# Retention attention with routed experts: routing intermediates in PSUM, the order of early weights, and the last two accumulating scatters

## The chip, the cores and the metric

One core of one Trainium2 chip runs the kernel, in one launch. The metric is device time in microseconds (us), lower is better. Engines carry the names of the profile: PE is TensorE, DVE is VectorE, ACT is ScalarE, POOL is GpSimd, SP is SyncE, which here only issues DMAs.

## The reference

```python
def _attn_ref(q, k, v):                      # (8, 8, 576, 64) each
    B, H, S, D_ = q.shape
    scores = 1.0 / np.sqrt(D_) * np.matmul(q, k.transpose(0, 1, 3, 2))
    gamma = 1.0 - 2.0 ** (-5.0 - np.arange(H, dtype=np.float32))
    rel = np.arange(S)[:, None] - np.arange(S)[None, :]
    Dmat = np.where(rel >= 0, gamma[:, None, None] ** rel[None, :, :], 0.0)
    return np.matmul(scores * Dmat[None], v)

def _moe_ref(x, w_gate, w_noise, noise, w1, w2):   # x (4608, 512), 8 experts, F = 1024
    noisy = x @ w_gate + np.log1p(np.exp(x @ w_noise)) * noise
    top2 = np.argpartition(-noisy, 2, axis=1)[:, :2]
    top2_w = softmax(noisy[top2])                  # over the two
    for e in range(8):
        for k in range(2):
            mask = top2[:, k] == e
            out[mask] += top2_w[mask, k, None] * (np.maximum(x[mask] @ w1[e], 0) @ w2[e])
```

The attention output, token by token, is `x` of the second part.

## The kernel before, in words

Nothing is scheduled by hand line by line. The class `Plan` holds a list of operations; each names its engine (or a choice of engines) with a cost in microseconds, what it reads and writes, and a priority. `Plan.run` simulates the engines with those costs and picks again and again the operation that can start first; among those that could start at the same time the lower `prio` goes first. Buffers are taken from pools in that simulation too. The outcome is one fixed order of instructions on each engine. On the chip every engine follows its order strictly: an instruction whose input is late holds everything behind it on that engine.

**Attention.** Sixteen units `u`, four for each pair of batches `bp`. `load` and `load_tail` fetch float32 q, k, v by DMAs that SP issues, `cast` scales and casts them to bf16 (k on ACT or DVE, line 501 or 503; q and v on DVE or POOL, lines 510 and 517), `tr` transposes on PE, `scores` and `states` multiply, `out_` finishes. `tail` handles the last 64 tokens of each batch.

**Routing.** After the four units of a pair, `route(bp)` computes the gates of its 1152 tokens on columns of 9, finds the two best experts, ranks tokens within each expert, and builds the table `xi` of token rows by expert: two one-hot tensors `olo` (18 x 128) and `oh` (18 x 80), made by comparing an iota with `lof` and `hif` (line 846), `oh` scaled by `vals` (849), and 18 matmuls (854). All its small tensors lie in SBUF, and some of its operations may go to POOL (the lists `DP` and `DC`). It also writes x with its gate values (`pay`) to `xd` in DRAM (line 886, issued by SP).

**Experts.** A piece is 128 rows of one expert (the tenth is 64). `tiles` closes 15 of the 80 pieces early, out of the tokens of the first three pairs (`CLOSE`), so that they can run while attention goes on; they are the tiles with `up` (line 1070) and the matmuls of line 1158. The other tiles, four pieces at most, follow in the main stage (`wide`, lines 1096 and 1158, the second matmul of one tile between the first ones of the next). `fetch` gathers rows of `xd` (POOL, line 993) two tiles ahead and transposes them on PE (line 1015), or by DMA transposes that SP issues (line 1005) from expert 5 on. `finish` scales the sum by its gate value (ACT at line 1192 or DVE at 1194) and scatters rows to the output (POOL, line 1198): a plain write for the lower-numbered of a token's two experts, an accumulating one for the other. Every token gets exactly these two. All of expert 7's rows are of the second sort, and its pieces 9 (64 rows) and 8 (128 rows), in this order, are the last tile.

**Weights.** Those of experts 0, 1 and 2 are cast by POOL's own DMAs (`weights` with `cast_dma`, lines 926 and 930), into space in which attention's raw inputs lay; `WAIT` names the unit whose loads must have landed first, and the priorities are 40, 41 and 42. Those of the other experts come as float32 through SP's DMAs (lines 940 and 943) and are cast by ACT or DVE (lines 282 and 284).

Two details of the end: before the last tile's finish there is a `drain` of POOL (line 1307), and behind everything a loop over tokens without room (`overflow`), which here runs zero times.

Of the kernel before, what the change touches and what calls it, by code (L numbers as in the profile page):

```python
# [17 lines left out]
P = 128  # L18
# [32 lines left out]
class Op:  # L51
    __slots__ = ("i", "eng", "fn", "prio", "dma", "port", "preds", "succ", "need", "allocs", "bufs", "fin", "on", "pace", "slack", "hold")


class Plan:
# [22 lines left out]
    def op(self, eng, cost, fn, r=(), w=(), prio=0.0, dma=0, after=(), port=False, pace=0.0, slack=0.0, hold=0.0):  # L78
        o = Op()
        o.i, o.fn, o.prio, o.dma, o.port, o.pace, o.slack, o.hold = len(self.ops), fn, prio, dma, port, pace, slack, hold  # L80
        o.eng = eng if isinstance(eng, dict) else {eng: cost}
# [30 lines left out]
    def run(self):  # L112
# [35 lines left out]
        while ready:  # L148
            pick = None
            for o in ready:  # L150
# [92 lines left out]
class Kernel:  # L243
# [47 lines left out]
    def setup(self):  # L291
# [87 lines left out]
        vals = f("vals", [P, 2 * C9, 2], F16)  # L379
        o("POOL", 0.2, vals, lambda: G.iota(vals.t.rearrange("p (j c) x -> p j c x", j=2), pattern=[[0, 2], [P, C9], [0, 2]],  # L380
# [10 lines left out]
        early = f("early", [P, 3, E])  # L391
# [3 lines left out]
        for e in range(E):  # L395
# [4 lines left out]
            for k in range(3):  # L400
                z(early, (k, e), early.t[:, k, e:e + 1], float(CLOSE[k][e] - FIRST[e]))
# [83 lines left out]
    def cast(self, u):  # L485
# [18 lines left out]
        for c in range(2):  # L504
            pl.op({"ACT": 0.63, "DVE": 0.43}, 0, lambda e, c=c: k(e, c), r=[(rk[c], x4)], w=[(kn, c)], prio=u, port=True)
# [217 lines left out]
    def route(self, bp, prio):  # L723
# [7 lines left out]
        def o(e, cost, fn, r, w, prio=prio):  # L731
            two = not {"tensor_reduce", "reciprocal", "tensor_single_scalar"} & set(fn.__code__.co_names)
# [8 lines left out]
        gv = lambda: pg.t[:, :C * 2 * E].rearrange("p (c e) -> p c e", c=C)  # L741

# [8 lines left out]
        nl = f("nl", [P, C, E])  # L751
        o("ACT", 0.23, lambda e: nc.scalar.activation(nl.t, gv()[:, :, E:], Act.Exp), [pg], [nl])
        o("ACT", 0.3, lambda e: nc.scalar.activation(nl.t, nl.t, Act.Ln, bias=1.0), [nl], [nl])
        o(DC, 0, lambda e: self.eng(e).tensor_tensor(nl.t, nl.t, nz.t[:, bp], Alu.mult), [nl, nz], [nl])
        o("DVE", DV, lambda e: V.tensor_add(nl.t, nl.t, gv()[:, :, :E]), [nl, pg], [nl])
# [6 lines left out]
        w = lambda j: keep_w.t[:, j, c0:c0 + C]  # L762

        def first_max(src, name):
            m, s, x = f(name + "m", [P, C]), f("scr", [P, C, E]), f(name + "w", [P, C])
            o("DVE", DV, lambda e: V.tensor_reduce(m.t, src.t, AX, Alu.max), [src], [m])
            o("DVE", DV, lambda e: V.tensor_tensor(s.t, src.t, bc(m.t), Alu.is_ge), [src, m], [s])
            o(DC, 0, lambda e: self.eng(e).tensor_tensor(s.t, s.t, dsc(), Alu.mult), [s, desc], [s])
            o("DVE", DV, lambda e: V.tensor_reduce(x.t, s.t, AX, Alu.max), [s], [x])
            return m, x  # L770

        m1, w1 = first_max(nl, "a")
        M1, nl2 = f("M1", [P, C, E]), f("nl2", [P, C, E])
        o("DVE", DV, lambda e: V.tensor_tensor(M1.t, dsc(), bc(w1.t), Alu.is_equal), [w1, desc], [M1])
        o("DVE", DV, lambda e: V.scalar_tensor_tensor(nl2.t, M1.t, -1.0e30, nl.t, Alu.mult, Alu.add), [M1, nl], [nl2])
        m2, w2 = first_max(nl2, "b")
# [4 lines left out]
        kw = [(keep_w, (bp, 0)), (keep_w, (bp, 1))]  # L781
        o("DVE", 0.3, lambda e: V.tensor_tensor(
            MM.t, desc.t.unsqueeze(1).unsqueeze(1).to_broadcast(sh),
            keep_w.t[:, :, c0:c0 + C].unsqueeze(3).to_broadcast(sh), Alu.is_equal), kw + [desc], [MM])

        d, r, x, df = f("d", [P, C]), f("r", [P, C]), f("low1", [P, C]), f("df", [P, C])
        pay = f(f"pay{bp % 2}", [P, C, PLW])
        tok = self.fixed["tok"]
        sub = lambda e, o_, a, b, op: self.eng(e).tensor_tensor(o_, a, b, op)
        o(DP, 0, lambda e: sub(e, d.t, m2.t, m1.t, Alu.subtract), [m1, m2], [d])  # L790
        o("ACT", 0.22, lambda e: nc.scalar.activation(d.t, d.t, Act.Exp), [d], [d])
        o(DP, 0, lambda e: self.eng(e).tensor_scalar_add(r.t, d.t, 1.0), [d], [r])
        o("DVE", DV, lambda e: V.reciprocal(r.t, r.t), [r], [r])
        o(DP, 0, lambda e: sub(e, d.t, d.t, r.t, Alu.mult), [d, r], [d])
        o("DVE", DV, lambda e: sub(e, x.t, w1.t, w2.t, Alu.is_gt), [w1, w2], [x])
        o(DP, 0, lambda e: sub(e, df.t, r.t, d.t, Alu.subtract), [r, d], [df])
        o(DP, 0, lambda e: sub(e, df.t, df.t, x.t, Alu.mult), [df, x], [df])
        o(DP, 0, lambda e: sub(e, pay.t[:, :, 0], d.t, df.t, Alu.add), [d, df], [(pay, 0)])
        o(DP, 0, lambda e: sub(e, pay.t[:, :, 1], r.t, df.t, Alu.subtract), [r, df], [(pay, 1)])
        o(DP, 0, lambda e: self.eng(e).tensor_copy(pay.t[:, :, 2].bitcast(I32), tok.t[:, bp]), [tok], [(pay, 2)])  # L800
# [4 lines left out]
        def ranks(e):  # L805
# [5 lines left out]
        o("PE", 0.9, ranks, [MM, ltri, ones], [pr])  # L811
        base, bnd, early = self.fixed["base"], self.fixed["bnd"], self.fixed["early"]
        ub, bt = f("ub", [P, 2, C, E]), f("bt", [P, 2, C])
        o(DP, 0, lambda e: self.eng(e).tensor_tensor(ub.t, MM.t, bnd.t.unsqueeze(2).to_broadcast(sh), Alu.mult), [MM, bnd], [ub])
        o("DVE", 0.3, lambda e: V.tensor_reduce(bt.t, ub.t, AX, Alu.add), [ub], [bt])
        u = f("u", [P, 2, C, E])
        o("DVE", 0.3, lambda e: V.tensor_tensor(u.t, rv()[:, :, :C, :], base.t.unsqueeze(2).to_broadcast(sh), Alu.add),
          [pr, base], [u])
        o("DVE", DV, lambda e: V.tensor_tensor(base.t, base.t, rv()[:, :, C, :], Alu.add), [pr, base], [base])
        if bp < 3:  # L820
            o("DVE", DV, lambda e: V.tensor_tensor(base.t[:, 0], base.t[:, 0], early.t[:, bp], Alu.max), [base, early], [base])
        o("DVE", 0.3, lambda e: V.tensor_tensor(u.t, u.t, MM.t, Alu.mult), [u, MM], [u])
        t = lambda: keep_t.t[:, :, c0:c0 + C]
        kt = (keep_t, bp)
        o("DVE", 0.3, lambda e: V.tensor_reduce(t(), u.t, AX, Alu.add), [u], [kt])
# [603 lines left out]
```

## Time and profile before

| | us |
|---|---|
| median of 3 runs (lowest to highest) | 442.14 (441.96 to 443.67) |
| the profiled execution: its time, its span | 438.85, 437.2 |
| PE busy in the span | 378.9 |
| POOL, ACT, DVE busy | 298.1, 263.3, 161.9 |
| mean granted clock of TensorE | 0.955 |

The span runs from the first to the last instruction. Spans and busy times are from one profiled execution, which was 3.29 us below the median of the runs. Rows of the profile give the line of the kernel, the engine, the operation, what it writes and reads, its duration, and in brackets how long the engine had been idle before it and which instruction's end it had been waiting for.

### The profile page before, as it was taken

The page shows a single profiled execution, that of the slowest core. Times are in us where ns is not written, and L with a number is a line of the kernel's source. Part 1 is how long each engine was busy: PE and PEld are TensorE (multiplying, and loading weights), DVE is VectorE, ACT ScalarE, POOL GpSimd, SP SyncE. Part 2 cuts the span into 40 slices and gives each one's busy share as a digit, 9 for nine tenths or more (in the row PEclk, how much of TensorE's full clock was granted, in tenths as well). Part 3 has the DMA queues.
Part 4 walks back from the last instruction along what each step waited for, and adds up shares of the span by engine and source line. Part 5 has one row for each costly group of instructions (what it writes and reads, how often), then busy time and mean ns, then how long its engine had stood idle before and what let it go on. Part 6 is the DMA issues. An engine that isn't in the chain of part 4 may idle for free. (4 is left out here: it accounts for less than half of the span.)

```text
span 437.2 us, 11020 instructions
## 1 busy us (share of the span) xinstructions
PE 378.9 (87%) x4312; PEld 240.4 (55%) x4312; DVE 161.9 (37%) x425; ACT 263.3 (60%) x450; POOL 298.1 (68%) x344
## 2 busy tenths in 40 slices
PE   2787686585989699999899898999999899999991
PEld 1675575574767567675465444554554454454460
DVE  4755489877477968002063403121102100000000
ACT  4688597744978454666657464465755464555451
POOL 8773787593489857575566667686786776783653
PEclk9999698876999699999999999999999999999997
DMA  8997999999993999973689859459999999697586
GB/s 236 300 259 172 312 266 259 309 263 251 286 266 59 235 230 205 343 273 114 251 288 311 264 154 273 145 106 251 176 290 197 291 187 166 125 135 114 74 108 81
DMA packets 99960, 94.26 MB, mean 216 GB/s; under 512 B 36799, under 2 KB 77248, under 8 KB 99906
## 3 DMA queue, kind: packets, MB, share of 16 engines
q1 hardware_dynamic: 82114, 58.08, 48.3%
q0 software_dynamic: 17792, 35.46, 40.4%
q8 instruction: 34, 0.56, 0.5%
q14 instruction: 20, 0.16, 0.1%
HBM read 72.32 MB, written 26.36 MB: 226 GB/s over the span
## 5 line engine op out<-in xcount | busy, mean ns | idle before, releaser
L1158 PE MATMUL ps<-W,half 128*128 128x512 bf16 x576 | 186.2, 379 | 2.9 <-ACT half L1079 2.6
L1096 PE MATMUL ps<-big,W 128*128 128x512 bf16 (+4 forms) x640 | 182.5, 329 | 0.0
L1079 ACT ACTIVATE half<-ps 128x512 bf16<-128x512 f32 (+5 forms) x188 | 93.5, 504 | 95.3 <-PE ps L1096 79.9
L1198 POOL DMA_INDIRECT out_dram<-half,xg x74 | 97.7, 1320 | 43.1 <-ACT half L1192 14.3
L993 POOL DMA_INDIRECT xg<-xd,xi x80 | 84.3, 1054 | 59.6 <-issue 15.6
L1158 PEld LDWEIGHTS <-half 128*128 128x128 bf16 x576 | 55.8, 98 | 63.0 <-ACT half L1079 3.3
L1096 PEld LDWEIGHTS <-W 128*128 128x128 bf16 x640 | 62.5, 98 | 46.4 <-issue 1.0
L1192 ACT ACTIVATE half<-ps,xg 128x512 f32<-128x512 f32 (+1 forms) x58 | 39.3, 678 | 12.9 <-PE ps L1158 11.6
L1194 DVE TENSOR_SCALAR half<-ps,xg 64x256 f32<-64x256 f32 (+1 forms) x24 | 14.0, 591 | 89.1 <-ACT half L1079 40.5
L572 DVE TENSOR_TENSOR half<-ps,mask 128x512 bf16<-128x512 f32 x64 | 40.1, 681 | 15.3 <-PE ps L564 11.4
L282 ACT ACTIVATE half<-ps 128x1024 bf16<-128x1024 bf16 (+1 forms) x35 | 34.8, 1011 | 12.3 <-PE ps L533 4.9
L284 DVE CAST W<-big 128x1024 bf16<-128x1024 f32 x25 | 17.2, 735 | 64.6 <-PE ps L1168 28.9
L1070 PE MATMUL ps<-half,W 128*128 128x256 bf16 (+1 forms) x288 | 29.9, 260 | 4.5 <-DVE half L284 4.4
L1070 PEld LDWEIGHTS <-W 128*128 128x128 bf16 x288 | 24.6, 99 | 8.5 <-issue 4.7
L282 ACT ACTIVATE tb<-ps 64x512 bf16<-64x512 f32 x32 | 18.9, 591 | 15.1 <-PE ps L597 14.9
L282 ACT ACTIVATE xT<-ps 128x512 bf16<-128x512 f32 (+1 forms) x37 | 18.6, 553 | 9.8 <-PE ps L642 6.7
L1015 PE MATMUL ps<-ident__61,xg 128*128 128x128 bf16 (+1 forms) x200 | 17.6, 219 | 4.8 <-DMA xg<-xd,xi 4.8
L597 PE MATMUL ps<-half,half 64*64 64x64 bf16 (+2 forms) x512 | 19.6, 228 | 2.3 <-POOL half L517 2.3
L533 PE MATMUL ps<-ident__61,half 128*128 128x128 bf16 x128 | 12.5, 255 | 10.2 <-POOL half L510 7.2
L564 PE MATMUL ps<-half,half 64*64 64x128 bf16 x512 | 12.9, 244 | 9.1 <-ACT half L282 8.8
L1015 PEld LDWEIGHTS <-xg 128*128 128x128 bf16 (+1 forms) x200 | 13.0, 98 | 12.5 <-DMA xg<-xd,xi 5.3
L597 PEld LDWEIGHTS <-half 64*64 64x64 bf16 (+1 forms) x512 | 16.6, 123 | 5.7 <-issue 3.6
(171 smaller groups left out, 444.9 us busy)
## 6 DMA issues: line engine op xcount, KB each, us to landing
big<-in_moe_w_dram SPq DMA_DIRECT2D x40, 512.0 KB, 7.3
W<-in_moe_w_dram POOLq DMA_DIRECT2D x12, 512.0 KB
xd<-xg SPq DMA_DIRECT2D x16, 264.0 KB, 6.3
W<-in_q_dram SPq DMA_DIRECT2D x16, 256.0 KB, 5.0
big<-in_k_dram SPq DMA_DIRECT2D x8, 512.0 KB, 5.8
big<-in_v_dram SPq DMA_DIRECT2D x8, 512.0 KB, 8.1
big<-in_q_dram SPq DMA_DIRECT2D x16, 256.0 KB, 7.1
W<-in_k_dram SPq DMA_DIRECT2D x6, 512.0 KB, 6.3
```

Of the source, the lines that this page charges most:

```text
L282: self.nc.scalar.activation(out, in_, Act.Copy)
L284: self.eng(e).tensor_copy(out, in_)
L572: nc.vector.tensor_tensor(S.t.bitcast(BF16).rearrange("p (h c x) -> p h c x", h=2, c=2)[:, h], p[h].t.rearrange("p (c x) -> p c x", c=2), ...
L597: nc.tensor.matmul(o[h * HD:(h + 1) * HD, hp, n, :], lhsT=kk[:k, r, c, y], rhs=vv[:k, r, c, y].unsqueeze(1).to_broadcast([k, n.stop - n.st ...
L993: ins = nc.gpsimd.indirect_dma_start(out=x.t[:n, :], out_offset=None, in_=self.xd[:rows, :], in_offset=IOff(ap=xi.t[:n, h:h + 1], axis=0), ...
L1015: nc.tensor.transpose(pv()[:, di, a:a + n], xb[:, di * P:(di + 1) * P], ident.t[:n, :n])
L1070: nc.tensor.matmul(pv()[:, f2, :], lhsT=w.t[:, o:o + P], rhs=xv()[:, di, :n], start=(di == 0), stop=(di == KD - 1))
L1079: self.nc.scalar.activation(o, i, Act.Relu)
L1096: self.mm = nc.tensor.matmul(p.t[:, :n], lhsT=w.t[:, o:o + P], rhs=xv()[:, di, :n], start=(di == 0), stop=(di == KD - 1))
L1158: self.mm = self.nc.tensor.matmul(po.t, lhsT=hv[:, c:c + P], rhs=self.W[e].t[:, o:o + DM], start=(f == 0), stop=(f == KF - 1))
L1192: nc.scalar.activation(y.t[:n, c], x, Act.Copy, scale=g()[:n])
L1198: ins = nc.gpsimd.indirect_dma_start(out=self.out[:, :], out_offset=IOff(ap=ix()[:n], axis=0), in_=y.t[:n, :], in_offset=None, bounds_chec ...
```

## The change

- **Routing.** Most small tensors of `route` move from SBUF into the PSUM tiles `pg` and `pr` that the logits and the ranks already use, in such a way that each instruction of DVE has at least one operand there. So both tiles stay taken through the route. All choices between DVE and POOL go to DVE, but for the product `ub` and one copy, which are POOL's. The one-hots compare the SBUF iota with PSUM columns, and are costed 2.47, 1.57 and 1.57 us instead of 1.36, 0.92 and 0.92. A route's priority goes from `u - 0.4` to `u + 1.1`.
- **Cast of k.** ACT only.
- **Early weights.** Experts 1 and 2 get priority 14.6 and 14.7 instead of 41 and 42.
- **Planned landings.** The plan takes a gather to land 3 us later for the DMA transposes that read it, and 5 us later for PE's transposes in the main stage.
- **The end.** For the two pieces of the last tile, `before` gathers the output rows that they will add to, behind all first writes; `finish` adds them in one DVE instruction, and the scatter is a plain one that waits for no other write.

The diff, cut to its core (of `route` only the parts that stand for the others):

```diff
@@ Plan.run
-                        t = max(t, p.fin + (o.hold + self.LAT if p.dma else 0.0 if p.on == e else self.LAT))
+                        t = max(t, p.fin + (o.hold + self.LAT if p.dma else 0.0 if p.on == e else self.LAT + o.late))
@@ cast
-            pl.op({"ACT": 0.63, "DVE": 0.43}, 0, lambda e, c=c: k(e, c), r=[(rk[c], x4)], w=[(kn, c)], prio=u, port=True)
+            pl.op({"ACT": 0.63}, 0, lambda e, c=c: k(e, c), r=[(rk[c], x4)], w=[(kn, c)], prio=u, port=True)
@@ route
-        DP = {"DVE": 0.19, "POOL": 0.3}
-        DC = {"DVE": 0.19} if bp % 2 else DP
+        wide = lambda i: pg.t[:, (2 + i) * C * E:(3 + i) * C * E].rearrange("p (c e) -> p c e", c=C)
+        thin = lambda i: pg.t[:, 5 * C * E + i * C:5 * C * E + (i + 1) * C]
+        nl, scr = ((lambda i=i: wide(i)) for i in range(2))
+        w1, m2, d, r, df = ((lambda i=i: thin(i)) for i in range(5))
...
-            o("DVE", DV, lambda e, j=j, op=op: V.tensor_tensor(w(j), w1.t, w2.t, op), [w1, w2], [(keep_w, (bp, j))])
+            o("DVE", DV, lambda e, j=j, op=op: V.tensor_tensor(kw(j), w1(), w2.t, op), ww, [at(("kw", j))])
...
-        o("DVE", DV, lambda e: V.tensor_single_scalar(ov.t, t(), 0.0, op=Alu.is_ge), [kt], [ov])
+        o("DVE", DV, lambda e: V.tensor_single_scalar(ov(), t(), 0.0, op=Alu.is_ge), [(pr, "t")], [(pr, "u"), (pr, "ov")])
+        o("ACT", 0.22, lambda e: nc.scalar.activation(val(), self.fixed["vals"].t.rearrange("p (j c) -> p j c", j=2), Act.Copy),
+          [self.fixed["vals"], (pr, "lo")], [(pr, "val")])
...
-        for dst, src, n, c in ((olo, lof, P, 1.36), (oh, hif, NH, 0.92)):
+        for dst, src, k, n, c in ((olo, lof, "lof", P, 2.47), (oh, hif, "hif", NH, 1.57)):
...
-        o("PE", 0.7, table, [olo, oh], [pT])
+        pl.op("PE", 1.3, table, r=[olo, oh], w=[(pT, 0)], prio=prio, late=0)
@@ fetch
-                    r=[x], w=[(xT, s)], prio=prio, dma=1.1)
+                    r=[x], w=[(xT, s)], prio=prio, dma=1.1, hold=3)
...
-                pl.op("PE", 0.25, tr, r=[x, ident], w=[(p, s)], prio=prio)
+                pl.op("PE", 0.25, tr, r=[x, ident], w=[(p, s)], prio=prio, hold=5 if early == 3 else 0)
@@ finish
-        y = pl.buf("half", "exp")
+        y = d.get("y", {}).get(s)
+        held = y is not None
+        y = y or pl.buf("half", "exp")
...
+                if held:
+                    nc.vector.scalar_tensor_tensor(y.t[:n, c], x, g()[:n], y.t[:n, c], Alu.mult, Alu.add)
...
-            self.scats.setdefault(i, []).append(pl.op("POOL", 1.8, lambda _: scat(second, True), r=[y] + src + rd,
+            self.scats.setdefault(i, []).append(pl.op("POOL", 1.3 if held else 1.8, lambda _: scat(second, not held),
+    def before(self, i, t, s, prio):
...
+        def get(_):
+            ins = nc.gpsimd.indirect_dma_start(
+                out=y.t[:n, :], out_offset=None, in_=self.out[:, :], in_offset=IOff(ap=second()[:n], axis=0),
+                bounds_check=N - 1, oob_is_err=False).ins
...
+            self.behind_firsts(ins, e)
+        pl.op("POOL", 1.3, get, r=[src] + [self.outk[x] for x in self.outk if x < e], w=[y], prio=prio, dma=0.9)
@@ record
-                pr = u - 0.4
+                pr = u + 1.1
...
-            self.weights(e, 40 + e, True, landed(u) + [o for b in pl.fifo[raw] for o in b.ops])
+            self.weights(e, (40, 14.6, 14.7)[e], True, landed(u) + [o for b in pl.fifo[raw] for o in b.ops])
...
+                for s in range(len(po) - 2, len(po)):
+                    self.before(i - 1, ts[-1], s, pr - 8)
```

More of the change, by code (lines that the diff above doesn't have):

```diff
@@ L51 @@
 class Op:
-    __slots__ = ("i", "eng", "fn", "prio", "dma", "port", "preds", "succ", "need", "allocs", "bufs", "fin", "on", "pace", "slack", "hold")
+    __slots__ = ("i", "eng", "fn", "prio", "dma", "port", "preds", "succ", "need", "allocs", "bufs", "fin", "on", "pace", "slack", "hold", "late")
 class Plan:
@@ L793, in route @@
[L793 to L799, printed above, removed]
@@ L822, in route @@
[L822 to L825, printed above, removed]
-        gli = f("gli", [P, 2, C], I32)
-        for j, op in ((0, Alu.add), (1, Alu.subtract)):
-            o("DVE", DV, lambda e, j=j, op=op: V.tensor_tensor(gli.t[:, j], bt.t[:, j], t()[:, j], op), [bt, kt], [(gli, j)])
-        lo, hi, lof, hif = f("lo", [P, 2, C], I32), f("hi", [P, 2, C], I32), f("lof", [P, 2, C, 2], F16), f("hif", [P, 2, C, 2], F16)
@@ L1203, in scat @@
             if add:
-                for x in range(e):
-                    for w in self.firsts[x]:
-                        tc.add_manual_dep(ins, w.name, mybir.DependencyInfo(
-                            mybir.DependencyClass.Sync, mybir.DependencyReason.DATA), reason="rows of the first expert")
-            else:
+                self.behind_firsts(ins, e)
+            elif not held:
                 self.firsts[e].append(ins)
```

161 lines of the change are left out of this document (100 added, 61 removed).

## The prediction

> **What bounds the kernel now.** I began with the page's head and a table of busy time by stage, because the chain that ended last holds only the final scatter here and tells nothing of the 430 us ahead of it.
>
> ```profile
> span 437.2 us, 11020 instructions
> 50.00:100.00 50.00, 37.45 (x938) 32.18 (x931) 43.49 (x87) 37.10 (x61) 39.26 (x57) 0.83 1.07 280
> 100.00:110.00 10.00, 6.55 (x119) 5.29 (x118) 7.21 (x16) 4.37 (x8) 2.38 (x4) 0.66 1.19 235
> 110.00:140.00 30.00, 27.85 (x534) 20.73 (x530) 18.62 (x37) 25.76 (x43) 23.41 (x25) 1.00 0.81 214
> 140.00:150.00 10.00, 6.68 (x171) 5.51 (x168) 9.21 (x19) 4.01 (x7) 9.23 (x20) 0.76 0.97 196
> 150.00:184.00 34.00, 32.91 (x384) 25.05 (x384) 19.86 (x61) 19.21 (x35) 21.35 (x31) 0.97 1.05 249
> 355.00:428.00 73.00, 72.90 (x419) 36.95 (x416) 1.92 (x4) 38.48 (x75) 48.25 (x37) 1.00 0.80 123
> ```
>
> Columns of the stages: from and to, length, busy time of PE, PE's weight loads, DVE, ACT and POOL, then granted clock, DMA share and GB/s. From 150 us on PE is busy without a break worth the name. So from there the end is the work that is left plus a tail. Time can come from three places: holes of PE before 150 us (the 15 early pieces are there to fill them, so a hole that goes makes the rest begin sooner), holes in the main stage, and what follows the last matmul. Before 100 us the DMA share is 1.07 and DVE is busy 43 of 50 us, so a freed engine there mostly waits for the loads; I expect nothing from that stretch. The holes by name are in the waits of PE (engine, line, waited for: total, times, longest), from 100 to 200 us, then from 200 to 432 us:
>
> ```profile
> PE ps L1070 <- DVE half L284: 4.4, 1, 4.4
> PE ps L632 <- DVE half L572: 1.7, 2, 1.4
> PE ps L597 <- POOL half L517: 1.6, 1, 1.6
> ...
> PE ps L1015 <- DMA xg<-xd,xi: 4.8, 5, 1.5
> PE ps L1158 <- ACT half L1079: 2.6, 1, 2.6
> ```
>
> **Route: what goes.** Why was DVE late at 103 and at 146 us? Its timeline, with one row of POOL between, then the same instructions undisturbed, and last the shortest, median and longest of line 572 in ns:
>
> ```profile
> 98.02 2.08 DVE L821 TENSOR_TENSOR base<-base,early 128x8 f32<-128x8 f32 x1
> 98.14 1.92 POOL L510 TENSOR_TENSOR half<-big,tabq 128x1024 bf16<-128x1024 f32 x1
> 101.36 1.07 DVE L832 TENSOR_SCALAR lo<-gli 128x18 int32<-128x18 int32 x1
> 102.71 0.68 DVE L284 COPY half<-ps 128x1024 bf16<-128x1024 bf16 x1
> 142.72 3.30 DVE L835 TENSOR_SCALAR ov<-keep_t 128x18 f32<-128x18 f32 x1
> ...
> 141.21 0.19 DVE L821 TENSOR_TENSOR base<-base,early 128x8 f32<-128x8 f32 x1
> 165.79 0.18 DVE L835 TENSOR_SCALAR ov<-keep_t 128x18 f32<-128x18 f32 x1
> 166.31 0.18 DVE L832 TENSOR_SCALAR lo<-gli 128x18 int32<-128x18 int32 x1
> ...
> L572 DVE TENSOR_TENSOR half<-ps,mask x64: 630/681/693, 11.4 to 147.6; 128x512 bf16<-128x512 f32 x64
> ```
>
> Eight numbers for a partition took 2.08 us instead of 0.19, and ended as POOL's product did. The stretched rows all have their operands in SBUF. DVE's 64 rows of line 572, with one operand in PSUM, all lie between 630 and 693 ns, so a route with an operand in PSUM in each instruction should run undisturbed. Line 284 at 102.71 stood behind such rows and held PE 4.4 us. Without the surplus of the two, 2.08 - 0.19 + 1.07 - 0.18 = 2.8 us, PE's hole shrinks by as much: **-2.8**. At 142.72 the surplus is 3.1 us, and the evictions of line 572 behind it cost PE 1.7 us; PE's 1.6 us behind POOL's line 517 I halve, since POOL loses the route's small products but keeps the rest: 1.7 + 0.8, **-2.5**.
>
> The clock was 0.66 in 100 to 110 us and 0.76 in 140 to 150 us, that is 6.8 and 4.8 us at half speed (twice the missing share). With PE busy in two thirds of both, full speed would give (6.8 + 4.8) / 2 x 0.66 = 3.8 us. Smaller holes may or may not prevent it. Bounds 0 and -3.8; I take **-1.5**, nearer to nothing, as other holes can bring such a stretch elsewhere.
>
> **Route: what it costs.** Groups, with mean ns behind the busy time:
>
> ```profile
> L572 DVE TENSOR_TENSOR half<-ps,mask 128x512 bf16<-128x512 f32 x64 | 40.1, 681 | 15.3 <-PE ps L564 11.4 <-POOL ltri L355 2.7 <-ACT nl L752 1.1
> L846 DVE TENSOR_TENSOR olo<-iota,lof 128x2304 f16<-128x2304 f16 x4 | 6.2, 1560 | 0.0
> L849 DVE TENSOR_TENSOR oh<-oh,vals 128x1440 f16<-128x1440 f16 x4 | 3.6, 907 | 0.1
> L846 DVE TENSOR_TENSOR oh<-iota,hif 128x1440 f16<-128x1440 f16 x4 | 3.6, 899 | 0.0
> L817 DVE TENSOR_TENSOR u<-ps,base 128x144 f32<-128x144 f32 x4 | 1.2, 300 | 0.1
> L503 DVE TENSOR_SCALAR half<-big 128x512 bf16<-128x512 f32 x5 | 4.8, 963 | 0.0
> L501 ACT ACTIVATE half<-W 128x512 bf16<-128x512 f32 x16 | 9.8, 636 | 0.9 <-DMA W<-in_k_dram 0.7
> ```
>
> A one-hot with a PSUM operand is not in the trace. Two PSUM rows give the slope: (681 - 300) / (512 - 144) = 1.035 ns for an element. So `olo` takes 300 + 2160 x 1.035 = 2.54 us and each pass over `oh` 300 + 1296 x 1.035 = 1.64 us: 5.82 instead of 1.56 + 0.90 + 0.91 = 3.37 us, +2.45 a route, +9.8 for four. Some ten small products that POOL carries today also go to DVE, about 0.2 us each (the row of line 789), and two copies and a second reciprocal are new: some 2.6 us a route, but DVE no longer waits for POOL between them. Queued behind all of it on DVE are evictions that PE waits for. Bounds 0 (PE has early pieces) and +9.8, as the small ones replace waits; I take **+1.5**, since from 110 to 140 us PE has little room and the last route has slack, as follows. Its rows of `xd` let the first gather of the main stage go at 181.08 us, and PE begins line 1096 at 199.08:
>
> ```profile
> 181.08 0.99 POOL L993 DMA_INDIRECT xg<-xd,xi  x1 [1.10 <-DMA xd<-xg]
> 199.08 1.11 PE L1096 MATMUL ps<-big,W 128*128 128x448 bf16 x5
> 139.28 0.83 POOL L926 DMA_DIRECT2D W<-in_moe_w_dram  x1
> 171.72 0.21 POOL L789 TENSOR_TENSOR df<-r,d 128x9 f32<-128x9 f32 x1
> PE ps L564 <- ACT half L282: 8.8, 8, 2.0
> ```
>
> Of those 18 us four gathers take 4 x (0.99 + 0.30) = 5.2, and landing and transposes, an estimate, as much again; some 8 us are to spare, more than 2.45.
>
> `pg` and `pr` now stay taken through a route, two of eight PSUM banks that attention drew on before. The last row above (waits of PE before 100 us) is how attention's evictions hold PE today; doubling it, +8.8, is my upper bound, 0 the lower. I take **+1.5**, near the lower one, as a route's lower priority also gives attention the first place on DVE and leaves the loads ahead of the `xd` writes in SP's queue.
>
> **The cast of k.** Five casts of 963 ns leave DVE, and ACT gets 5 x 0.64 = 3.2 us. ACT was busy 37.10 of 50 us where most of them are; that idle time covers it. 0, or +3.2 without the cover.
>
> **Early weights.** Expert 1's first DMA went at 139.28 us behind POOL's attention work. From 110 to 140 us the DMA share is 0.81, so an earlier start has room. What it can fill is PE's other holes there, 30 - 27.85 = 2.15 us; it can also put four DMA issues ahead of q and v casts on POOL, at 0.83 us each. Bounds -2.2 and +3.3; I take **-0.5**.
>
> **Main stage.** The 4.8 us for gathers are five waits of at most 1.5 us by transposes that the plan had put too early. With 5 us more in the plan they fall into place; the danger is a transpose so late that line 1096 waits for `xT`. I take four fifths, **-3.8** (bounds -4.8 and 0). DMA transposes planned later let SP's weight loads go ahead, which could remove the 2.6 us, or make a transpose late by as much: 0, bounds -2.6 and +2.6.
>
> **The end.** Start, duration, line and idle time of the last scatters, a plain one beside them, and two stages after the last issue (columns as above):
>
> ```profile
> 426.12 1.54 POOL L1198 DMA_INDIRECT out_dram<-half,xg  x1 [0.89 <-ACT half L1192]
> 427.96 1.42 POOL L1198 DMA_INDIRECT out_dram<-half,xg  x1 [0.30 <-issue]
> 427.98 0.69 ACT L1192 ACTIVATE half<-ps,xg 128x512 f32<-128x512 f32 x1 [0.92 <-ACT half L1192]
> 429.69 1.56 POOL L1198 DMA_INDIRECT out_dram<-half,xg  x1 [0.30 <-POOLq L1319]
> ...
> 252.21 1.00 POOL L1198 DMA_INDIRECT out_dram<-half,im  x1 [0.30 <-issue]
> ...
> 431.30:434.20 2.90, 0.00 (x0) 0.00 (x0) 0.00 (x0) 0.00 (x0) 0.00 (x0) 0.59 0.78 102
> 434.20:437.20 3.00, 0.00 (x0) 0.00 (x0) 0.00 (x0) 0.00 (x0) 0.00 (x0) 0.50 0.02 5
> ```
>
> POOL issues three scatters back to back; the last two become plain at 1.00 us instead of 1.42 and 1.56, which is -1.0. The addition on DVE takes what ACT's scaling took (0.69). The transfer runs 2.9 us after the issue; a write that need not read its target saves between 0 and 2.9, and I take 1.2, below half. The 3.0 us at the close stay. **-2.2**. The two new gathers (0.99 + 0.30 us each, as at 181.08) have to fit into POOL's gaps ahead of that, such as the 0.89 us before 426.12; without gaps they would cost 2.6 us.
>
> **Sum.** -2.8 - 2.5 - 1.5 + 1.5 + 1.5 - 0.5 - 3.8 - 2.2 = -10.3 us. The profiled execution took 438.85 us, 3.29 less than the median of the runs, 442.14. It would take 428.55; with the same distance the median is **431.8**. 0.5% (2.2 us) is about what a measurement of this kernel can tell from no change.
>
> **Rivals.** *The front gives nothing.* The stalls go, but the longer one-hots and fewer banks give it back, so that the early pieces end when they did. For it: DVE's busy share of 0.87 in 50 to 100 us. Against it: the two holes have one cause each, seen in the rows. Main stage and end remain: 442.14 - 6.0 = 436.1.
>
> *The one-hots lie on PE's path* (the slow end). If all 9.8 us hold evictions that PE waits for and the stalls, being waits that PE would have had anyway, give nothing, it is 442.14 + 9.8 - 6.0 = 445.9. It decides from 2.05 us a route, (6.0 + 2.2) / 4. For it: DVE is in order, and its busy time in 140 to 150 us is 9.21. Against: in three of four routes PE has pieces to work on. The Trainium skill, VectorE: DVE Perf Modes, Rules for kernel authors, advises against this change: accept full-length passes on PSUM or copy to SBUF first if many operations follow. By that rule the route loses, as in this rival; the stretched rows above speak for the change.
>
> *The clock stays full.* If holes under the present ones no longer bring half speed, the whole 3.8 comes: 431.8 - 2.3 = 429.5. For it: both half stretches follow the two holes that shrink. Against: the 0.83 of 50 to 100 us has many small holes only. The Trainium skill, TensorE: Matmul & The Clock Gate, Part 1, says that the gate judges PE by free-running windows; by that the stretch could as well move as go, and the trace cannot tell.
>
> *The stalls stay,* because it is not the SBUF operands that expose DVE to POOL: 442.14 + 1.5 + 1.5 - 0.5 - 6.0 = 438.6. Against: the 64 rows of line 572, none above 693 ns.
>
> **How the numbers follow.** Forecast 0.44, front gives nothing 0.25, one-hots on the path 0.15, full clock 0.10, stalls stay 0.06. The range goes from 421 (the bounds of PE's hole at 103 us, the clock, the weights, the main stage and the end together give -1.6 - 2.3 - 1.7 - 1.0 - 2.6 - 1.7 = -10.9 more) to 444, where the one-hots expose four fifths (436.1 + 7.9); about 0.13 lie above and 0.05 below. Faster by over 0.5%: all of the forecast and the clock, most of the second case and half of the last: 0.77. Slower: 0.16. Within: 0.07.
>
> **What would show it.** Right: no route row of DVE far over its shortest; one-hots of about 2.5 and 1.6 us; PE's wait of 4.4 us at line 1070 under 2; line 926 for expert 1 well before 139 us; PE's waits at line 1015 after 200 us under 1; the last scatters at 1.0 us. Wrong: PE's waits on line 572 or 282 grown by more than 5 us in all; line 1096 waiting for `xT`; the main stage beginning after 199 us.

## The result, and the profile after

The changed kernel took 430.18 us (median of 6 runs, 424.03 to 435.16) against 442.23 us (439.74 to 443.67): ratio 0.966, 95% interval 0.959 to 0.974. The ratio leaves out two of the changed kernel's runs, 433.58 and 435.16 us, that fell in a slower state; the two medians alone give 0.973. The forecast, 431.8 us, lies 1.6 us from the median, but its largest terms were wrong in opposite directions, as the experiments show. The profiled execution took 424.86 us, nearly the fastest of the runs, against 438.85 us before; they lie 5.3 and 3.4 us below their medians. Both are used for where the time lies, and the medians for how much it is.

The head of the page, the table by stage (columns as in the prediction) and the first matmul of the main stage:

```profile
span 423.3 us, 11033 instructions
...
50.00:100.00 50.00, 33.74 (x774) 28.91 (x775) 41.72 (x112) 33.10 (x58) 37.40 (x43) 0.75 1.07 280
100.00:110.00 10.00, 9.38 (x230) 7.88 (x231) 6.69 (x14) 8.29 (x13) 1.40 (x2) 0.87 1.02 229
110.00:140.00 30.00, 27.23 (x514) 20.37 (x515) 23.25 (x57) 23.29 (x41) 26.26 (x30) 1.00 1.01 257
140.00:150.00 10.00, 8.94 (x293) 7.69 (x293) 6.07 (x15) 8.58 (x15) 7.37 (x8) 1.00 1.17 253
150.00:184.00 34.00, 32.15 (x304) 22.90 (x302) 17.86 (x56) 19.72 (x39) 20.03 (x25) 1.00 0.93 273
184.00:262.00 78.00, 78.00 (x571) 46.01 (x570) 21.87 (x50) 50.89 (x88) 54.04 (x50) 1.00 0.71 233
262.00:345.00 83.00, 83.00 (x481) 42.77 (x480) 12.37 (x25) 50.44 (x89) 61.38 (x52) 1.00 0.92 226
345.00:355.00 10.00, 10.00 (x52) 4.72 (x49) 0.00 (x0) 5.49 (x11) 7.87 (x6) 1.00 1.04 150
...
196.09 0.92 PE L1113 MATMUL ps<-big,W 128*128 128x448 bf16 x4
```

The same table of the kernel before, for the stretches that the prediction didn't show:

```profile
184.00:262.00 78.00, 74.61 (x542) 43.48 (x540) 18.38 (x40) 48.03 (x85) 49.88 (x46) 1.00 0.73 241
262.00:345.00 83.00, 81.51 (x473) 41.12 (x468) 17.95 (x38) 45.95 (x79) 60.03 (x52) 1.00 0.92 214
345.00:355.00 10.00, 7.38 (x47) 3.94 (x46) 0.00 (x0) 6.32 (x12) 7.10 (x6) 1.00 1.18 234
```

From 184 to 355 us PE had 7.5 us of holes before and has none now (3.39 + 1.49 + 2.62). Three parts can be read off. The main stage begins 3.0 us earlier, at 196.09. From there to the end of the last matmul it takes 219.65 us instead of 228.82, that is 9.2 less: 7.5 of holes, and 1.7 of PE's own busy time. Of the 200 matmuls that transpose gathered rows, 112 lie in this stage instead of 119, and PE is busy with them for 8.32 us instead of 10.60. From the last matmul to the close there are 7.56 us instead of 9.34, 1.8 less. Together that is 14.0 us.

The first part is the least certain. If the main stage and the end are equally long in each execution, the medians leave 12.05 - 9.2 - 1.8, about 1 us, for the front; that is an estimate.

Inside the front, PE is 4.5 us busier than before from 100 to 150 us, with the granted clock at 0.87 and 1.00 in the two stretches that stood at 0.66 and 0.76. But in 50 to 100 us it is 3.7 us less busy than the 37.45 of before, at a clock of 0.75 instead of 0.83. The low clock moved; it did not go. The mean over the run is 0.952 against 0.955.

The whole front, before and after, then PE's first table in the changed kernel (the matmuls of line 867 for the first route), its wait at the early `up` before 100 us, the wait at the first table of before, and two stretches with a low clock in the changed kernel:

```profile
0.00:199.08 199.08, 157.50 (x2973) 124.91 (x2973) 124.90 (x349) 131.78 (x215) 140.74 (x215) 0.91 0.97 250
0.00:196.09 196.09, 155.06 (x2976) 122.89 (x2977) 123.72 (x387) 135.02 (x227) 134.30 (x186) 0.90 0.97 256
...
67.57 1.38 PE L867 MATMUL ps<-oh,olo 128*128 128x80 f16 x18 [5.24 <-DVE keep_t L851]
...
PE ps L1087 <- DMA W<-in_moe_w_dram: 3.0, 1, 3.0
...
PE ps L854 <- DVE oh L849: 2.1, 1, 2.1
...
65.00:70.00 5.00, 2.43 (x52) 2.15 (x54) 4.89 (x9) 1.65 (x2) 0.34 (x2) 0.51 0.91 209
95.00:100.00 5.00, 1.69 (x8) 1.06 (x9) 4.97 (x5) 0.60 (x1) 1.73 (x2) 0.50 1.18 206
```

Ahead of the main stage PE stands idle for 41.0 us (196.09 - 155.06), against 41.6 before (199.08 - 157.50). So the holes of the front moved and hardly shrank. The new ones lie before 100 us: 5.2 us at the first table, behind DVE's one-hots, where it was 2.1, and 3.0 us for weights. The clock is low at both of these waits, 0.51 and 0.50.

The one-hots (groups), the waits of PE from 100 to 200 us, and the first weight DMA of expert 1:

```profile
L860 DVE TENSOR_TENSOR olo<-iota,ps 128x2304 f16<-128x2304 f16 x4 | 10.2, 2554 | 1.0 <-ACT ps L849 0.9
L862 DVE TENSOR_TENSOR oh<-oh,ps 128x1440 f16<-128x1440 f16 x4 | 6.6, 1654 | 0.1
L860 DVE TENSOR_TENSOR oh<-iota,ps 128x1440 f16<-128x1440 f16 x4 | 6.6, 1648 | 0.0
...
PE ps L753 <- issue: 1.1, 2, 0.6
PE ps L867 <- DVE oh L862: 1.0, 1, 1.0
PE ps L816 <- DVE MM L789: 1.0, 2, 0.5
...
129.05 1.54 POOL L943 DMA_DIRECT2D W<-in_moe_w_dram  x2
```

The wait of 4.4 us at the early `up` behind DVE (line 1070, now 1087) is gone, and expert 1's weights are asked for 10.2 us earlier. After 200 us PE waits for nothing: no wait on line 1032 (1015 before) is left. The end, with POOL's first scatter behind the drain, the last matmul, the held addition of line 1211 and the last scatters:

```profile
388.16 1.56 POOL L1219 DMA_INDIRECT out_dram<-half,xg  x1 [7.64 <-ACT half L1096]
...
413.84 1.90 PE L1175 MATMUL ps<-W,half 128*128 128x512 bf16 x8
413.92 1.56 POOL L1219 DMA_INDIRECT out_dram<-half,xg  x1 [0.80 <-ACT half L1213]
415.78 0.75 DVE L1211 SCALAR_TENSOR_TENSOR half<-ps,xg,half 128x512 f32<-128x512 f32 x1 [0.80 <-PE ps L1175]
415.78 0.98 POOL L1219 DMA_INDIRECT out_dram<-half,xg  x1 [0.30 <-issue]
417.06 1.02 POOL L1219 DMA_INDIRECT out_dram<-half,xg  x1 [0.31 <-DVEq L1363]
```

Lines shift with the edits: the early `up` is 1070 before, 1087 after and near it elsewhere, the second matmul 1158 and 1175, the one-hots' table 854 and 867, the scatter 1198 and 1219. The same program spreads over 11 us from run to run, so an edit worth 2 us shows in the rows and not in the times. Below, "to before" is the ratio to runs of the kernel before on the same chip, with its 95% interval; begin, length and tail are those of the main stage in the profiled execution, read like the three parts above. The kernel before took 438.9 to 441.0 us (medians) beside these versions, against 442.2 us beside the changed kernel, which was not run again with them. So a version can be level with the changed kernel in us and 1% behind it in the ratio, and where the two disagree the runs do not decide.

### The profile page after: what moved, and what is told of

It is laid out like the page before. It is cut to its first block, busy times and chain, and to the rows that moved or that the text cites. A ratio compares the mean times of both kernels' runs of the same rounds, so it can differ in the third digit from the quotient of the medians.

```text
span 423.3 us, 11033 instructions
## 1 busy us (share of the span) xinstructions
PE 374.7 (89%) x4312; PEld 238.6 (56%) x4312; DVE 160.1 (38%) x463; ACT 265.1 (63%) x460; POOL 290.0 (69%) x314
## 5 line engine op out<-in xcount | busy, mean ns | idle before, releaser
L1010 POOL DMA_INDIRECT xg<-xd,xi x80 | 83.2, 1040 | 56.8 <-issue 19.9
L1219 POOL DMA_INDIRECT out_dram<-half,xg x74 | 95.3, 1288 | 33.9 <-ACT half L1096 12.2
L1213 ACT ACTIVATE half<-ps,xg 128x512 f32<-128x512 f32 (+1 forms) x59 | 39.5, 669 | 13.1 <-PE ps L1175 12.5
L1215 DVE TENSOR_SCALAR half<-ps,xg 128x512 f32<-128x512 f32 (+1 forms) x20 | 12.2, 612 | 86.1 <-ACT half L1213 32.5
L285 DVE CAST W<-big 128x1024 bf16<-128x1024 f32 x22 | 14.9, 726 | 35.6 <-PE ps L1185 24.7
L520 POOL TENSOR_TENSOR half<-big,tab 128x512 bf16<-128x512 f32 x16 | 16.6, 1048 | 4.2 <-DMA big<-in_v_dram 4.2
L1219 POOL DMA_INDIRECT out_dram<-half,im x12 | 16.3, 1358 | 3.7 <-issue 2.7
L536 PE MATMUL ps<-ident__61,half 128*128 128x128 bf16 x128 | 11.5, 242 | 7.7 <-POOL half L513 4.6
```

The source lines that it names most:

```text
L285: self.eng(e).tensor_copy(out, in_)
L520: self.eng(e).tensor_tensor(o, i, t, Alu.mult)
L1010: ins = nc.gpsimd.indirect_dma_start(out=x.t[:n, :], out_offset=None, in_=self.xd[:rows, :], in_offset=IOff(ap=xi.t[:n, h:h + 1], axis=0), ...
L1213: nc.scalar.activation(y.t[:n, c], x, Act.Copy, scale=g()[:n])
L1219: ins = nc.gpsimd.indirect_dma_start(out=self.out[:, :], out_offset=IOff(ap=ix()[:n], axis=0), in_=y.t[:n, :], in_offset=None, bounds_chec ...
```

## Experiments: which part carries the main stage

**Both holds away from the changed kernel** (`e1_no_hold`).

```diff
-                    r=[x], w=[(xT, s)], prio=prio, dma=1.1, hold=3)
+                    r=[x], w=[(xT, s)], prio=prio, dma=1.1)
-                pl.op("PE", 0.25, tr, r=[x, ident], w=[(p, s)], prio=prio, hold=5 if early == 3 else 0)
+                pl.op("PE", 0.25, tr, r=[x, ident], w=[(p, s)], prio=prio)
```

> The changed kernel with both planned landings taken back (the plan again takes a gather to land at its usual time for the transposes). Theory A, the planned landings alone close PE's holes in the main stage: PE waits again for gathers at the transposes and perhaps once for late weights, 4 to 8 us in all after 190 us, and the time rises by as much over the changed kernel's 430.2. Theory B, the holes closed because the route and the weights come earlier and gathers have a better start: those waits stay under 1 us and the time does not move.

Measured: 429.56 us (424.25 to 430.98), 0.982 (0.973 to 0.990) to before; begin 195.73, length 219.1, tail 7.82. PE has no listed wait after 203 us. The holes do not come back without the holds: Theory B.

**Only the hold of 3 away** (`e2_pe_hold_only`): the first half of the diff above.

> The changed kernel with the 3 us for the DMA transposes taken back and the 5 us for PE's transposes kept. Theory A (each hole has its own planned landing): PE's waits for gathers at the transposes stay at 0, and one wait of 2 to 3 us for ACT behind a late weight load comes back near expert 6's first tile. Theory B (the weight hole was closed by something else, such as the earlier start): no wait comes back, and the time does not move.

Measured: 428.94 us (425.7 to 431.58), 0.978 (0.967 to 0.988); begin 201.76, length 219.65, tail 7.36. No wait came back after 203 us: Theory B. Length and tail are those of the changed kernel and the begin is 5.7 us later. Ahead of the main stage the traces of the two show the same order of instructions on every engine, so these 5.7 us are a spread between executions and not the work of the edit. The front's 3.0 us of the profiled pair are less than this spread.

**The two holds alone, on the kernel before** (`e3_before_holds`): the edit of `e1_no_hold` the other way round.

> The kernel before with the two planned landings as the only change. Theory A: PE's holes after 200 us, 7.6 us, go to under 1, and the time falls by 5 to 8 us from 442.2, to 434 to 437. Theory B (they need the earlier route or weights): holes of 4 us or more stay and the time falls by less than 3.

Measured: 433.89 us (431.15 to 436.68), 0.990 (0.985 to 0.995); begin 202.25, length 221.54, tail 10.15. The only wait of PE after 203 us:

```profile
PE ps L1096 <- ACT big L282: 1.0, 1, 1.0
```

The main stage is 7.3 us shorter than before. So the holds do what the prediction said when they are alone, the 2.6 us behind ACT goes too, and in the changed kernel something else does the same work. The next two runs say what.

## Experiments: the route

**The old route in the changed kernel** (`e4_old_route`): `route` with all it needs from before (operands in SBUF, small products shared with POOL), planned at the changed place.

> The changed kernel with the route of before (small tensors in SBUF, part of them on POOL, short one-hots), at the new priority. Theory A (the route in PSUM is what the front gains by): DVE's stretched rows come back, some 20 us in all, the main stage begins 2 to 5 us later, and the time rises by 2 to 5 us over the changed kernel's 430.2. Theory B (the longer one-hots and the two banks cost what the stalls did): no change within 2 us, or a gain.

Measured: 429.11 us (427.35 to 430.28), 0.977 (0.973 to 0.982); begin 197.06, length 220.3, tail 10.43. Stretched rows are back: summed over DVE's rows of the route, what lies above the shortest row of the same line and shape is 13.1 us (19.1 in the kernel before, 0.6 in the changed one). The loss that Theory A gave them, 2 to 5 us, does not show in the times: 429.11 against 430.18 us, and a begin 1.0 us later. By the ratios, 0.977 against 0.966, a cost of about 1% is not excluded.

**The new route alone, on the kernel before** (`e5_new_route`): `route` and its constants from the change, planned at the old place, all else as before.

> The kernel before with the new route alone, at the old priority, without planned landings. Theory A: no stretched rows of DVE, the main stage begins 2 to 5 us earlier than at 199, and the time falls by 2 to 5 us from 440. Theory B: the front does not move, and what falls is only PE's holes of 7.5 us in the main stage, if the new order happens to close them. Both are told apart by where the main stage begins and how long it is (228.8 us before, 219.7 changed).

Measured: 444.43 us (439.33 to 449.74), 1.012 (1.006 to 1.017): slower by about 1%. Begin 209.3, length 219.1, tail 9.38. PE's first table, its longest wait from 100 to 200 us, and the stage behind that:

```profile
65.63 1.36 PE L866 MATMUL ps<-oh,olo 128*128 128x80 f16 x18 [10.26 <-DVE oh L861]
...
PE ps L1174 <- DMA W<-in_moe_w_dram: 4.7, 1, 4.7
...
150.00:184.00 34.00, 26.90 (x343) 19.38 (x340) 18.31 (x58) 17.54 (x33) 14.41 (x21) 0.97 0.96 236
```

The route in PSUM gains nothing by itself. PE stands 10.3 us at the first table behind the long one-hots (2.1 in the kernel before), and later it reaches the second matmul of an early piece before the weights. What each of the two waits costs was not tried apart. The length of 219.1 us, with no wait in it and no hold in the plan, is what stood in for the holds in `e1_no_hold`: a new route gives the planner another order, and in that order the transposes come late enough.

**Short one-hots in the changed kernel** (`e9_sbuf_onehots`): only the one-hots go back to f16 pairs in SBUF.

```diff
-        lof, hif, val = lambda: pair(356), lambda: pair(374), lambda: pair(392)
+        lof, hif = f("lof", [P, 2, C, 2], F16), f("hif", [P, 2, C, 2], F16)
...
-        for dst, src, k, n, c in ((olo, lof, "lof", P, 2.47), (oh, hif, "hif", NH, 1.57)):
+        for dst, src, n, c in ((olo, lof, P, 1.36), (oh, hif, NH, 0.92)):
```

> The changed kernel with one thing put back: the one-hots are compared against f16 pairs in SBUF as before the change, while the rest of the route stays in PSUM. Theory A (the one-hots lie beside PE's work, their length is on no path): the rows of olo and oh go back from 2554, 1648 and 1654 ns to about 1350, 900 and 910, so VectorE is busy 2.7 us less in each route, 10.8 us in all, and the time stays that of the changed kernel: ratio to the kernel before 0.96 to 0.98, PE's idle time ahead of the main stage 38 to 46 us, the table of the last route at about 164 to 168. Rival B (the +1.5 us of the prediction's sum, and its rival of one-hots on PE's path): each of the routes is 2.7 us earlier, PE's wait of 5.2 us at the second table goes to about 2.5, the main stage begins 1.5 to 4 us earlier and the ratio is 0.955 to 0.965. Rival C (the pairs in SBUF meet POOL's products again): one-hot or cast rows over 2 us stretched, some 1 to 3 us slower.

Measured: 430.22 us (426.75 to 437.75), 0.974 (0.967 to 0.981); begin 200.89, length 219.87.

```profile
L860 DVE TENSOR_TENSOR olo<-iota,lof 128x2304 f16<-128x2304 f16 x4 | 7.1, 1785 | 0.0
L863 DVE TENSOR_TENSOR oh<-oh,vals 128x1440 f16<-128x1440 f16 x4 | 3.6, 908 | 0.1
L860 DVE TENSOR_TENSOR oh<-iota,hif 128x1440 f16<-128x1440 f16 x4 | 3.6, 897 | 0.0
```

DVE is freed of 9.1 us (10.2 + 6.6 + 6.6 against 7.1 + 3.6 + 3.6), and no gain shows in the time: Theory A. One of the four `olo` was stretched, which is why the mean is 1785 and not 1350, but that is under 2 us of DVE's time. Rival B was right about the wait, though: PE's 5.2 us at the table (the first in time, which the text above calls the second) go to 0.5. But PE now waits 4.7 us for gathers (line 1033) between 100 and 200 us, and its idle time ahead of the main stage is 42.3 us (200.89 - 158.56) against 41.0. A wait that is taken away at one place comes back at another.

## Experiments: early weights and the place of the route

**Weights late again in the changed kernel** (`e6_late_weights`).

```diff
-            self.weights(e, (40, 14.6, 14.7)[e], True, landed(u) + [o for b in pl.fifo[raw] for o in b.ops])
+            self.weights(e, 40 + e, True, landed(u) + [o for b in pl.fifo[raw] for o in b.ops])
```

> The changed kernel with priorities 41 and 42 for the weights of experts 1 and 2 again. Theory A (earlier weights fill PE's holes before the main stage): expert 1's first weight DMA goes 5 us or more later than at 129, PE's holes from 100 us to the main stage grow by 2 to 4 us, and the time by as much. Theory B (the weights were not the limit there): under 1 us either way.

Measured: 440.17 us (436.52 to 451.91), 1.001 (0.997 to 1.004): all of the gain is lost. Begin 211.08, length 219.77, tail 7.5. PE's waits and the stage in which they fall:

```profile
PE ps L1175 <- DMA W<-in_moe_w_dram: 6.8, 2, 3.7
PE ps L753 <- issue: 2.9, 1, 2.9
...
150.00:184.00 34.00, 25.50 (x260) 19.80 (x260) 17.47 (x57) 16.04 (x28) 14.87 (x21) 0.90 0.98 252
```

**Route at its old place in the changed kernel** (`e7_route_first`).

```diff
-                pr = u + 1.1
+                pr = u - 0.4
```

> The changed kernel with the route's priority at u - 0.4 again. Theory A (a route behind attention keeps attention's evictions and SP's loads moving): PE's holes before the main stage grow, and the time rises by 1 to 4 us. Theory B (the order of the two does not matter, since the same work has to be done before the early pieces): under 1 us.

Measured: 436.32 us (434.07 to 439.2), 0.995 (0.991 to 0.998). Begin 204.3, length 220.2, tail 10.24. PE's waits from 100 to 200 us, and POOL's first scatter behind the drain:

```profile
PE ps L867 <- DVE oh L862: 4.6, 2, 3.4
PE ps L1032 <- DMA xg<-xd,xi: 1.7, 1, 1.7
...
408.78 1.59 POOL L1219 DMA_INDIRECT out_dram<-half,xg  x1 [7.71 <-issue]
```

With 3.4 us before 100 us PE stands 8.0 us at the tables, against 6.2 in the changed kernel. But 2.7 of the 6 us are the tail: POOL comes out of the drain only 15.7 us ahead of the last matmul's end, instead of 27.6.

**Early weights alone, on the kernel before** (`e11_before_early_w`): the edit of `e6_late_weights` the other way round.

> The kernel before with one part of the change alone: the weights of experts 1 and 2 are asked for ahead of the route. Theory A (the transfers of these weights set the front by themselves): the first weight DMA of expert 1 goes out 8 to 10 us earlier, at about 130, PE's wait of 4.4 us at the first product of expert 1 goes below 1, the main stage begins 3 to 6 us earlier (193 to 196 against 199) and still has its 7.5 us of waits, so the time is 4 to 6 us shorter, ratio 0.985 to 0.99. Rival B (the prediction's price of 0.5 us, or the kernel before doesn't need them, since its route comes first and its writes of k end late): main stage at 198 to 200, ratio 0.995 to 1.003. Rival C (the transfers ahead hold up the DMAs of the route and of the rows): PE waits for xd writes or gathers instead, 1 to 4 us slower, ratio 1.003 to 1.01.

Measured: 444.29 us (439.56 to 447.41), 1.006 (1.001 to 1.011): a little slower, as in Rival C. Begin 202.96, length 229.25, tail 10.01. The first weight DMA went at 135.68, 3.6 us earlier than before, and the waits are the old ones and some at the first gathers (from 100 to 200 us, then after 203):

```profile
PE ps L1070 <- DVE half L284: 3.7, 1, 3.7
PE ps L1015 <- DMA xg<-xd,xi: 2.6, 2, 2.4
...
PE ps L1015 <- DMA xg<-xd,xi: 3.4, 4, 1.8
PE ps L1158 <- ACT half L1079: 3.0, 1, 3.0
```

**Early weights and later route, on the kernel before** (`e13_before_pair`): both edits together, nothing else.

> The kernel before with two parts of the change alone: the route planned behind the next unit's work (1.1 instead of -0.4) and the weights of experts 1 and 2 asked for early; route in SBUF, k cast, holds and scatters as before. Theory A (these two carry the front, and only together, since early weights alone came out at 1.006 and each of them without the other in the changed kernel at 0.995 and 1.001): the main stage begins at 196 to 199 instead of 199 to 209, its length stays at about 228 with 7 to 8 us of holes, the tail at 9.3 to 10.4, so the time is 434 to 438, ratio 0.982 to 0.993. Rival B (the k cast on ScalarE or the holds are needed for the front too): main stage at 200 to 205, ratio 0.997 to 1.01. Rival C (the moved route also reorders the first gathers and closes the holes of the main stage without any hold): main stage under 222 us long with under 2.5 us of holes, ratio 0.97 to 0.98.

Measured: 435.6 us (432.74 to 436.44), 0.990 (0.984 to 0.996). The ratio is Theory A's, the place is not: begin 200.67, no earlier than before, but length 223.24 with 4.3 us of holes instead of 7.5, tail 10.19. The moved route closed part of the main stage's holes, by order alone, as in Rival C, though less than that said.

## Experiments: the end

**The last two pieces accumulate again** (`e8_adds_last`).

```diff
-                for s in range(len(po) - 2, len(po)):
-                    self.before(i - 1, ts[-1], s, pr - 8)
```

> The changed kernel with the last two pieces accumulating in their scatter as before, without the rows fetched ahead. Theory A (the plain scatters give the whole difference of the end): from the last matmul to the close it takes 9.3 us again instead of 7.6, and the rest is the same. Theory B (the end got shorter because POOL's backlog was shorter): it stays at about 7.6 to 8.

Measured: 428.68 us (427.09 to 434.47), 0.978 (0.969 to 0.986), level with `e2_pe_hold_only`, so the times can't tell. Its profiled execution took 434.47 us, 5.8 us above the median, and is read only for its last rows:

```profile
421.69 1.90 PE L1175 MATMUL ps<-W,half 128*128 128x512 bf16 x8
...
423.62 1.42 POOL L1219 DMA_INDIRECT out_dram<-half,xg  x1 [0.30 <-issue]
425.34 1.56 POOL L1219 DMA_INDIRECT out_dram<-half,xg  x1 [0.30 <-POOLq L1361]
```

The last issue ends 3.31 us after the last matmul (426.90 - 423.59), in the changed kernel 2.34 (418.08 - 415.74): 1.0 us, as predicted. The close behind it takes 6.0 us (432.9 - 426.90) instead of 5.2 (423.3 - 418.08). So the tail is 9.3 us again, as Theory A said, and the plain scatters give the whole 1.8 us of the end.

**Old route, and no drain on POOL** (`e12_old_route_no_drain`). In `e4_old_route` POOL comes out of the drain only 15.7 us ahead of the last matmul's end (27.6 in the changed kernel) and issues what has piled up back to back:

```profile
392.42 1.49 POOL L1203 DMA_INDIRECT out_dram<-half,xg  x1 [2.12 <-DVE half L1199]
401.62 1.60 POOL L1203 DMA_INDIRECT out_dram<-half,xg  x1 [7.70 <-issue]
403.52 1.57 POOL L1203 DMA_INDIRECT out_dram<-half,xg  x1 [0.30 <-issue]
...
421.22 1.04 POOL L1203 DMA_INDIRECT out_dram<-half,xg  x1 [0.30 <-issue]
```

That is the tail of 10.43 instead of 7.56 us. The edit:

```diff
-            if i == len(ts) - 1:
-                pl.op("POOL", 8.8, lambda _: self.nc.gpsimd.drain(), prio=pr - 20, after=[self.got])
```

> The changed kernel with the route of before (in SBUF, POOL sharing) at the changed place, as in the run with the old route, and now without the drain on POOL that is planned into the main stage behind the last gather. Theory A (POOL comes out of that drain at 401.6, 15.7 us ahead of the last matmul, and then has to issue nine scatters of 1.6 us back to back, so that the last two are late): without it no idle of 7.7 us on POOL, the scatters follow the evictions one by one, the tail after the last matmul goes from 10.4 to 7.4 to 8.0, and the time is 2.5 to 3 us shorter than that of the run with the old route: 426 to 427, ratio 0.968 to 0.973, so that it is level with the changed kernel or better. Rival B (what the drain waits for has to be waited for at the end in any case): the tail is 10 to 15 us, ratio 0.977 to 0.99. Rival C (the last gathers are late too, and POOL is full by itself): no long idle on POOL, the tail stays at 9.5 to 10.5, ratio 0.975 to 0.98.

Measured: 430.27 us (428.65 to 431.28), 0.977 (0.971 to 0.982); begin 197.26, length 220.3, tail 11.44. The last scatter and two stages of the close:

```profile
418.90 1.04 POOL L1203 DMA_INDIRECT out_dram<-half,xg  x1 [0.31 <-DVEq L1345]
...
423.00:426.00 3.00, 0.00 (x0) 0.00 (x0) 0.00 (x0) 0.00 (x0) 0.00 (x0) 0.50 0.01 5
426.00:429.00 3.00, 0.00 (x0) 0.00 (x0) 0.00 (x0) 0.00 (x0) 0.00 (x0) 0.50 0.00 0
```

The scatters follow the evictions one by one, as Theory A said, but the close after the last issue takes 9.1 us (429.0 - 419.94) instead of 5.5 in `e4_old_route`: Rival B. The close loses 3.5 us, more than the 2.5 us by which the last issue follows the last matmul sooner (2.4 us behind it instead of 4.9), so the tail grows from 10.43 to 11.44. Planned in ahead of the end, the drain lies beside matmuls. No version here is faster than the changed kernel by more than the spread of its runs (428.7 us is the lowest median), and by the ratio none is.

## Why the prediction was right, and where it was not

The direction and the total held; the shares did not, and that the total came so close is in good part luck. Predicted, then measured:

- **Route: what goes, -2.8 and -2.5.** The mechanism was right in the rows: no row of the route is stretched, and the wait of 4.4 us is gone. Its price was the wrong step. With the rows stretched again for 13.1 us, `e4_old_route` takes about the same time, and the new route alone is 1.2% slower. PE's idle time ahead of the main stage went only from 41.6 to 41.0 us: in the changed kernel PE waits longer at the first table and for the first weights instead, and in the new route alone 10.3 us at that table and 4.7 us for weights. I had subtracted two waits without asking what is late next in the order that the planner then writes.
- **Half clock, -1.5.** Nothing came of it: the clock rose where the holes had been (0.87 and 1.00) and fell in 50 to 100 us (0.75 instead of 0.83), where PE's waits now lie. The prediction had named this: other holes can bring such a stretch elsewhere. The Trainium skill, TensorE: Matmul & The Clock Gate, Part 1, says that the gate judges PE's activity by free-running windows; no run here shows the window itself.
- **Route: what it costs, +1.5 and +1.5.** The durations were right: 2554, 1648 and 1654 ns against 2.54 and 1.64 us. The one-hots do stand on PE's path at the first table, 5.2 us in the changed kernel and 10.3 us in the new route alone, as the rival said. But taking them away there gained nothing that the times show (`e9_sbuf_onehots`), so the rival's price of 9.8 us is out for the changed kernel. In the new route alone their price was not measured. Banks: attention's evictions hold PE 4.7 us before 100 us instead of 8.8; no cost of the banks shows in that row. The Trainium skill, VectorE: DVE Perf Modes, Rules for kernel authors, says to accept full-length passes on PSUM or to copy to SBUF first if many operations follow. With the compared columns in SBUF, DVE was indeed busy 9.1 us less, but no run here shows a shorter kernel by it.
- **Cast of k, 0.** Not tried alone. PE's waits on ACT's casts are 5.8 us (three), 5.1 before.
- **Early weights, -0.5.** The worst step. It was priced as filler for PE's holes. Alone it costs 2.7 us (0.6% of 441), within its bounds; in the changed kernel its absence costs 10 us (440.17 against 430.18), far outside. It has to be priced together with the other edits: it is what lets them keep their gain. The later place of the route had no term of its own in the sum, and in the changed kernel its absence costs 6 us, 2.7 of them at the tail (`e7_route_first`).
- **Main stage, -3.8 and 0.** Measured -9.2. The prediction's first reading, that PE has no break from 150 us on, passed over the 7.5 us of holes that this term then counts. The holds alone close the holes, as predicted, but they were not needed: the new route without any hold gives 219.1 us too. The 2.6 us at 350 us, put at 0 with bounds of 2.6, went in each version but `e11_before_early_w` and `e13_before_pair`. That PE's busy time in the stage fell by another 1.7 us was in no term; the transposes of gathered rows, 2.3 us less there, account for it in size.
- **The end, -2.2.** Measured -1.8 in the profile: 1.0 for the issues as predicted, and 0.8 behind the last issue where I had taken 1.2.

So the front gave 3 us of a predicted 4.3 in the profiled pair and about 1 us by the medians, by a balance of parts of other sizes than mine: `e2_pe_hold_only` began at 201.76 with the same order ahead of it. What sets the begin of a single run was not settled. The main stage gave 5.4 us more than predicted, which made up for it. In the medians, 12.05 us against 10.3.

## What to carry to other kernels

When the order comes out of a planner, an edit changes the order far from where it is made, so measure each part both ways, added alone and taken away: here early weights cost 0.6% in one kernel and were worth over 2% in the other. A wait in the profile has a price only after you have asked what is late behind it, and a stage table of each version (begin, length, holes, tail) tells that sooner than the total. List the waits of the whole run and not only of the stretch that the edit was meant for: here the holes that went after 100 us came back before it. A part too small for the total's spread of 11 us can still be settled by its own rows.

## What was not expected of the hardware

The drain on POOL left it idle for 7.64 us in the changed kernel and 7.70 in `e4_old_route`, and in `e12_old_route_no_drain`, without it, the close behind the last scatter grew by 3.5 us. The stretches with a low clock moved with PE's waits instead of going: with PE 4.5 us busier from 100 to 150 us, the mean granted clock of the run went from 0.955 to 0.952. And one order of instructions ahead of the main stage took 196.09 us in one execution and 201.76 us in another.
